# One weave of a two-layer SSM and MLP kernel reordered: halves of the w1T product in turn, the second H pair earlier, output sums first on VectorE

## The chip, the core and the metric

The kernel runs on one core of a Trainium2 chip. The metric is the device time of one execution in microseconds; less is better. The profile is of one execution, taken by the hardware profiler; times inside it count from the start of its span.

## What is computed

The reference runs a forward pass of two layers (each a state-space convolution block, then a two-matrix MLP with SiLU, both on a layer norm of the residual stream) and the gradients of all its weights and inputs but one:

```python
def _B_ref(x, w1, w2):
    return jnp.einsum("bsf,fd->bsd", _silu(jnp.einsum("bsd,df->bsf", x, w1)), w2)

x = A_q
x = x + _A_ref(_layernorm(x), A_k, A_v, A_shift_k, A_ssm_k, A_ssm_D)
x = x + _B_ref(_layernorm(x), B_w1, B_w2)
x = x + _A_ref(_layernorm(x), A_k, A_v, A_shift_k, A_ssm_k, A_ssm_D)
x = x + _B_ref(_layernorm(x), B_w1, B_w2)
# outputs: x and the vjp of x with respect to A_q, A_k, A_v, A_shift_k, A_ssm_k, A_ssm_D, B_w1, B_w2
```

There are 2048 tokens of width 448 and an inner width of 1792, all in bf16. Both layers use the same weights. `_A_ref` multiplies a layer-normed row by a convolution result y that both layers share, and adds it to the row.

## The kernel before

A prefix computes y by a matmul FFT, a main part (class `Main`) runs the two layers forward and back over four chunks of 512 tokens, and a suffix does the FFT backward, while a list of weight-gradient jobs fills the gaps. The change lies in the main part. In the code the first layer is `L = 0` and the second `L = 1`.

For a chunk the main part has these steps, each a generator that yields between pieces of TensorE work:

- `H` (line 809): the pre-activations w1 x nT in seven pairs of 128 rows, grouped 2, 3, 2 (`pairs`, line 680). The first call of a group does that pair's long products and the short "rests" (line 678) of all pairs of the group; each further call does one more pair. A pair sits in a PSUM buffer of tag `mm`, of which there are two; the fourth pair uses two buffers of tag `tr`. ScalarE reads a pair twice: SiLU into aT (line 817), and a copy into Dall (lines 818 and 116), from which `slope` (line 823) makes the derivative later. ScalarE loads a table ahead of the first SiLU and ahead of the first slope.
- `O` (line 829): for each of the chunk's four token tiles 14 matmuls of aT with w2 into a PSUM buffer of tag `po` (two buffers), in two halves of seven, then VectorE adds the sum to X (line 838). For the second layer, X goes out as the result and the upstream gradient is loaded in its place, two tiles at a time.
- `G` (line 844): the same shape as `H` with w2T and the gradient; ScalarE (and VectorE for the pairs in `dv`) evicts, and VectorE multiplies by the slope, giving the two halves of ghT (line 857, or line 980 for the second layer).
- `N` (line 860): for each of the four token tiles 14 matmuls of ghT with w1T into a `po` buffer, the first seven on ghT's first half and the last seven on its second, with a yield between; ScalarE reads the sum out into `lb_u0` (line 876), scaled, and VectorE runs two layer-norm backward steps (`_ln_bwd`, line 1027; lines 885 to 889). `lb_u0`, `lb_u1` and `gy` share three buffers of the tag `lb_u0`.
- `T` (line 894): transposes of a normed chunk on TensorE into `tr` buffers, copied to nT by ScalarE and VectorE in halves.

The order of TensorE's instructions is written out by hand (`manual_schedule` with the tensor engine alone): `weave` (line 904) takes a string and calls the named generators letter by letter. The order on VectorE, ScalarE, GpSimd and the DMA queues is made by the scheduler of the framework, which goes by program order as priority, by its own estimate of when operands are ready, and by marks: `high_priority()` puts instructions ahead of all others, `issue_after` behind a given one.

The loop over chunks (line 953) runs, for chunk c: O and G of layer 2; N of layer 2 with H of layer 1 for chunk c + 1; O of layer 1 for chunk c + 1; the forward gating and norms of layer 2 (`fwd1`, lines 768 to 777, norms from line 301 with `L308`, `L312`, `L313`, `L316`); G of layer 1; and then, for chunks 0 to 2, at line 1013, N of layer 1 with H of layer 2 for chunk c + 1:

```python
weave("NNTNNHNHNHNHNHHH", N=n, T=self.T(self.n1[1], nT, GBLK), H=self.H(c + 1, 1, nT, r))
```

In chunk 3 there is no next chunk, and N is woven with weight-gradient jobs.

## Time and profile before

| what | value |
|---|---|
| time, median of 3 runs (lowest, highest) | 695.97 us (693.32, 698.3) |
| the profiled execution's time | 692.97 us |
| its span | 690.9 us |
| TensorE matmul busy in the span | 669.0 us (97%) |
| VectorE, ScalarE, GpSimd busy | 481.6, 429.9, 104.8 us |
| granted TensorE clock | 0.999 of full |

A line of a timeline gives the start, the time until the last of its instructions ends, the engine, the line of the kernel, the operation, its output and inputs by the program's names, their sizes, and how many instructions are merged (x7). In brackets stands how long the engine had been idle before it and whose result ended that. Matmuls are pipelined: one starts well before the last has ended, so idle time in brackets is less than what the work lost, and the distance between starts says more.

| stretch of the profile before | us |
|---|---|
| N's first tile of chunk 0 to H's first step | 202.28 to 209.60 |
| H's first step to the end of the weave | 209.60 to 226.69 |
| the same two of chunk 1 start at | 293.86, 301.19 |
| and of chunk 2 | 385.45, 392.79 |

The weave takes 24.41 us in chunk 0 (202.28 to 226.69).

### The profile page before, as it was taken

To read this page: it belongs to the slowest core of one execution; us is meant where nothing else is said; L and a number is where in the kernel's file an instruction comes from. 1 tells how busy PE (TensorE), PEld (TensorE's weight loads), DVE (VectorE), ACT (ScalarE), POOL (GpSimd) and SP (SyncE) were. 2 spreads that over 40 slices of the span, in tenths; PEclk is the share of its full clock that TensorE was granted. 3 is DMA by queue.
4 is the path that set the end of the run, shared out by engine and by line. 5 is a ranking of instruction groups with operands and counts; after the bars stand their busy time and mean duration, and the time that the engine had idled before them with its cause. 6 is when DMAs were issued, how large, how long until landed. Compare 5 with 4: busy or idle time off the path is not lost.

```text
span 690.9 us, 14461 instructions
## 1 busy us (share of the span) xinstructions
PE 669.0 (97%) x5844; PEld 362.1 (52%) x5879; DVE 481.6 (70%) x1131; ACT 429.9 (62%) x522; POOL 104.8 (15%) x177
## 2 busy tenths in 40 slices
PE   8999999899999999999999999999999999999997
PEld 6876745454434444444444444544555555555666
DVE  5779943667889858899478874843936555538992
ACT  5988976878947868669577585223543543554431
POOL 1057310110011100111001000010111211102311
PEclk9999999999999999999999999999999999999999
DMA  8999978179698777597766789949599988957991
GB/s 320 244 316 321 337 203 220 56 191 259 167 265 233 221 182 176 137 253 219 199 157 183 211 231 354 271 142 210 191 249 342 328 285 315 341 190 223 320 310 42
DMA packets 203956, 162.60 MB, mean 235 GB/s; under 512 B 153505, under 2 KB 184244, under 8 KB 203122
## 3 DMA queue, kind: packets, MB, share of 16 engines
q1 hardware_dynamic: 190806, 113.35, 60.2%
q0 software_dynamic: 11088, 39.84, 16.7%
q10 hardware_dynamic: 1996, 8.49, 3.7%
q8 instruction: 46, 0.75, 0.5%
q14 instruction: 20, 0.16, 0.1%
HBM read 66.05 MB, written 54.60 MB: 175 GB/s over the span
## 4 chain that ended last, share of the span: by engine, by line
PE 64%; DVE 19%; issue 6%; ACT 5%; DMA 3%; POOL 3%; POOLq 0%; ACTq 0%
PE ps_d L1082 25%; PE ps_n L872 8%; PE ps_h L674 6%; PE ps_g L674 6%; PE ps_o L834 5%; DVE ln_st L308 2%; DVE lb_v L1030 2%; PE ps_v L272 2%; POOL rstd L313 2%; DMA spec_K<-KAB 1%; DVE n L316 1%; DVE lb_v L1033 1%; DVE lb_v L1034 1%; DVE X L838 1%; PE ps_h L678 1%
## 5 line engine op out<-in xcount | busy, mean ns | idle before, releaser
L1082 PEld LDWEIGHTS <-dstat 128*128 128x128 bf16 x928 | 87.1, 98 | 75.7 <-issue 4.0
L872 PE MATMUL ps_n<-w1T,ghT 128*128 128x448 bf16 x448 | 96.6, 353 | 2.0 <-DVE ghT L857 1.7
L834 PE MATMUL ps_o<-w2sb,aT 128*128 128x448 bf16 x448 | 89.2, 353 | 0.6 <-DVE X L838 0.6
L674 PE MATMUL ps_h<-nT,w1sb 128*128 128x512 bf16 (+1 forms) x410 | 83.5, 336 | 2.2 <-ACT Dall L116 1.0
L116 ACT CAST ghT<-ps_g 128x1024 bf16<-128x1024 f32 (+1 forms) x54 | 48.4, 900 | 58.3 <-PE ps_g L678 47.7
L674 PE MATMUL ps_g<-nT,w2T 128*128 128x512 bf16 x317 | 77.9, 379 | 2.2 <-DVE Dall L117 0.5
L872 PEld LDWEIGHTS <-ghT 128*128 128x128 bf16 x448 | 41.4, 98 | 50.7 <-DVE ghT L857 6.7
L834 PEld LDWEIGHTS <-aT 128*128 128x128 bf16 x448 | 43.2, 98 | 41.1 <-issue 2.7
L674 PEld LDWEIGHTS <-w1sb 128*128 128x128 bf16 x420 | 39.2, 98 | 36.7 <-issue 7.2
L817 ACT ACTIVATE aT<-ps_h 128x1024 bf16<-128x1024 f32 (+1 forms) x48 | 44.2, 921 | 19.1 <-PE ps_h L674 10.2
L1030 DVE SCALAR_TENSOR_TENSOR lb_v<-lb_u,n 128x448 bf16<-128x448 bf16 x60 | 37.2, 620 | 24.5 <-ACT lb_u L876 24.1
L116 ACT CAST Dall<-ps_h 128x1024 bf16<-128x1024 f32 (+2 forms) x60 | 54.3, 904 | 0.0
L313 POOL TENSOR_TENSOR rstd<-ln_ve,mhalf 128x2 f32<-128x2 f32 (+1 forms) x24 | 19.9, 831 | 225.7 <-DVE ln_ve L312 225.7
L674 PEld LDWEIGHTS <-w2T 128*128 128x128 bf16 x336 | 31.3, 98 | 42.1 <-issue 7.2
L827 ACT ACTIVATE Dall<-Dall 128x1024 bf16<-128x1024 bf16 (+1 forms) x48 | 53.2, 1186 | 0.1
L1082 PE MATMUL ps_d<-X,dstat 128*128 128x448 bf16 x224 | 47.6, 353 | 0.0
L1082 PE MATMUL ps_d<-go,dstat 128*128 128x448 bf16 x224 | 47.2, 353 | 0.0
L1082 PE MATMUL ps_d<-n3m,dstat 128*128 128x448 bf16 (+1 forms) x240 | 47.0, 340 | 0.0
L1082 PE MATMUL ps_d<-n1m,dstat 128*128 128x448 bf16 (+1 forms) x240 | 46.5, 340 | 0.0
L876 ACT ACTIVATE lb_u<-ps_n,rstd 128x448 bf16<-128x448 f32 x32 | 20.5, 640 | 28.9 <-PE ps_n L872 24.3
L116 ACT CAST A1g<-ps_v 128x1024 bf16<-128x1024 f32 x14 | 15.0, 1069 | 36.5 <-PE ps_v L272 36.5
L838 DVE TENSOR_TENSOR X<-X,ps_o 128x448 bf16<-128x448 bf16 x32 | 19.5, 611 | 21.3 <-PE ps_o L834 21.1
(210 smaller groups left out, 1112.4 us busy)
## 6 DMA issues: line engine op xcount, KB each, us to landing
dstat<-a_d SPq DMA_DIRECT2D x28, 512.0 KB, 5.2
dstat<-g_d SPq DMA_DIRECT2D x28, 512.0 KB, 5.8
a_d<-turned SPq DMA_DIRECT2D x16, 512.0 KB, 3.0
g_d<-turned SPq DMA_DIRECT2D x16, 512.0 KB, 3.0
a_d<-turned SPq DMA_DIRECT2D x16, 384.0 KB, 2.7
g_d<-turned SPq DMA_DIRECT2D x16, 384.0 KB, 3.0
spec_K<-KAB POOLq DMA_DIRECT2D x7, 512.0 KB, 5.7
KAB<-KAB POOLq DMA_DIRECT2D x28, 128.0 KB, 5.1
```

The lines of the kernel that those rows point to most:

```text
L116: return nc.scalar.copy(out, in_)
L272: nc.tensor.matmul(pv[:, r ^ (ci & 1), i, :], lhsT=src[ri, i * P:(i + 1) * P], rhs=k.Gsb[ri, g, ri], start=first, stop=not first)
L313: nc.gpsimd.tensor_tensor(out=r[:, lo:hi], in0=ve[:, lo:hi], in1=k.mhalf[:, lo:hi], op=ALU.pow)
L674: self.nc.tensor.matmul(ps, lhsT=w[:, b, ft * P:(ft + 1) * P], rhs=x[:, b], start=(start and b == 0), stop=(stop and b == bs[2]))
L817: self.last_silu = nc.scalar.activation(aT[hh][:, o:o + hi - lo, :], ps(lo, hi), ACT.Silu)
L827: self.nc.scalar.activation(dT[hh][:, o:o + n, :], dT[hh][:, o:o + n, :], ACT.Derivative_silu)
L834: nc.tensor.matmul(po[:, :D], lhsT=aT[ft // 7][:, ft % 7, tl * P:(tl + 1) * P], rhs=self.w2sb[:, ft, :], start=(ft == 0), stop=(ft == NF - 1))
L838: self.last_o = nc.vector.tensor_tensor(out=X[:, t, :], in0=X[:, t, :], in1=po[:, :D], op=ALU.add)
L872: nc.tensor.matmul(pn[:, :D], lhsT=gh[ft // 7][:, ft % 7, tl * P:(tl + 1) * P], rhs=self.w1T[:, ft, :], start=(ft == 0), stop=(ft == NF - 1))
L876: nc.scalar.activation(u0[:], pn[:, :D], ACT.Identity, scale=k.rstd[2 * L + 1][:, t:t + 1], accum_out=cp[:, tl, 0:1])
L1030: nc.vector.scalar_tensor_tensor(out=v[:], in0=u0, scalar=-1.0 / D, in1=n_t, op0=ALU.mult, op1=ALU.mult, accum_out=cp[:, 1:2])
L1082: self.nc.tensor.matmul(ps[:, cols], lhsT=st[:, t, :], rhs=mov[:, t, cols], start=(first and t == 0), stop=(last and t == NT - 1))
```

## The change

Three things change.

1. `N` gets an inner function `product(tl, h)` that does seven matmuls of tile tl with half h of ghT. For layer 1 (`L == 0`) in chunks 0 to 2 the first call does tile 0's first half, the second call tile 1's first half, the third tile 0's second half and the fourth tile 1's second half. The other tiles, layer 2 and chunk 3 go as before. There are eight calls in all, as before.
2. The string of the weave of layer 1's N with layer 2's H calls H's second step right after the first, and its sixth and seventh after the last N. With the first edit, TensorE's order from the start of the weave is: first half of tile 0, first half of tile 1, transposes, second half of tile 0, second half of tile 1, then two H steps.
3. In `O`, for the second layer and chunks 1 to 3, the sum into X is marked with `high_priority()`.

```diff
     def O(self, c, L, aT, tls=range(4)):
...
             t = 4 * c + tl
-            self.last_o = nc.vector.tensor_tensor(out=X[:, t, :], in0=X[:, t, :], in1=po[:, :D], op=ALU.add)
+            with tc.high_priority() if L == 1 and c > 0 else nullcontext():
+                self.last_o = nc.vector.tensor_tensor(out=X[:, t, :], in0=X[:, t, :], in1=po[:, :D], op=ALU.add)
...
     def N(self, c, L, gh, gres, n_b, n_a):
...
+        mix = L == 0 and c < 3
+        pns = {}
+
+        def product(tl, h):
+            if h == 0:
+                pns[tl] = k.psum.tile([P, 512], FP32, name="ps_n", tag="po", bufs=2)
+            for ft in range(7 * h, 7 * h + 7):
+                nc.tensor.matmul(pns[tl][:, :D], lhsT=gh[h][:, ft % 7, tl * P:(tl + 1) * P], rhs=self.w1T[:, ft, :], start=(ft == 0), stop=(ft == NF - 1))
+
         for tl in range(4):
...
-            pn = k.psum.tile([P, 512], FP32, name="ps_n", tag="po", bufs=2)
-            for ft in range(NF):
-                nc.tensor.matmul(pn[:, :D], lhsT=gh[ft // 7][:, ft % 7, tl * P:(tl + 1) * P], rhs=self.w1T[:, ft, :], start=(ft == 0), stop=(ft == NF - 1))
-                if ft == 6:
-                    yield
+            if not (mix and tl == 1):
+                product(tl, 0)
+                yield
+            if mix and tl == 0:
+                product(1, 0)
+                yield
+            product(tl, 1)
+            pn = pns.pop(tl)
             u0 = self.t([P, D], "lb_u0", "lb_u0", 3)
...
-                weave("NNTNNHNHNHNHNHHH", N=n, T=self.T(self.n1[1], nT, GBLK), H=self.H(c + 1, 1, nT, r))
+                weave("NNTNNHHNHNHNHNHH", N=n, T=self.T(self.n1[1], nT, GBLK), H=self.H(c + 1, 1, nT, r))
```

More of the change, by code (lines that the diff above doesn't have):

```diff
@@ L1 @@
-from contextlib import ExitStack
+from contextlib import ExitStack, nullcontext
 import numpy as np
@@ L829, in O @@
     def O(self, c, L, aT, tls=range(4)):
-        nc, k, X = self.nc, self.k, self.X
+        nc, k, X, tc = self.nc, self.k, self.X, self.tc
         for tl in tls:
```

## The prediction

> **What bounds the kernel now.** I read the page's first part, TensorE's timeline from the end of the layer-1 G product to the next G product, then VectorE and ScalarE there, then the same stretches of the next two chunks. Chunks 0, 1 and 2 of the weave that the change rewrites are called c0, c1 and c2; they start at 202.28, 293.86 and 385.45.

> ```profile
> span 690.9 us, 14461 instructions
> PE 669.0 (97%) x5844; PEld 362.1 (52%) x5879; DVE 481.6 (70%) x1131; ACT 429.9 (62%) x522; POOL 104.8 (15%) x177
> ```

> TensorE is the bound, but 97% hides its short waits: a matmul lasts 0.353 us and the next starts after 0.19, so a gap shows only when starts are compared. Its timeline in c0:

> ```profile
> 202.28 1.49 PE L872 MATMUL ps_n<-w1T,ghT 128*128 128x448 bf16 x7
> 204.08 0.36 PE L872 MATMUL ps_n<-w1T,ghT 128*128 128x448 bf16 x1 [0.32 <-DVE ghT L857]
> 204.68 1.75 PE L872 MATMUL ps_n<-w1T,ghT 128*128 128x448 bf16 x6 [0.24 <-DVE ghT L857]
> 206.37 0.64 PE L651 MATMUL ps_t<-ident,n 64*128 64x64 bf16 x32
> 206.94 2.82 PE L872 MATMUL ps_n<-w1T,ghT 128*128 128x448 bf16 x14
> 209.60 1.46 PE L674 MATMUL ps_h<-nT,w1sb 128*128 128x512 bf16 x5
> ...
> 224.27 0.39 PE L678 MATMUL ps_h<-nT,w1sb 64*128 64x512 bf16 x2
> 225.05 0.39 PE L678 MATMUL ps_h<-nT,w1sb 64*128 64x512 bf16 x2 [0.40 <-ACT Dall L116]
> 225.38 1.47 PE L674 MATMUL ps_h<-nT,w1sb 128*128 128x512 bf16 x6
> ```

> Three things are to be seen: the second half of N's first tile (204.08, 204.68) waits for ghT; the sixth H step (its last two rests, 225.05) waits for a PSUM buffer of the mm tag; and between them TensorE runs without a gap. Who is late, on VectorE and then on ScalarE:

> ```profile
> 202.99 0.70 DVE L316 TENSOR_SCALAR n<-X,ln_mv,rstd 128x448 bf16<-128x448 bf16 x2 [0.59 <-POOL rstd L313]
> 203.61 2.22 DVE L857 TENSOR_TENSOR ghT<-Dall,ghT 128x512 bf16<-128x512 bf16 x4
> ...
> 209.66 0.35 DVE L1034 TENSOR_TENSOR lb_v<-lb_v,lb_u 128x448 bf16<-128x448 bf16 x1
> ...
> 233.62 0.61 DVE L838 TENSOR_TENSOR X<-X,ps_o 128x448 bf16<-128x448 bf16 x1
> ```

> ```profile
> 206.52 0.63 ACT L876 ACTIVATE lb_u<-ps_n,rstd 128x448 bf16<-128x448 f32 x1 [3.04 <-PE ps_n L872]
> ...
> 210.12 0.63 ACT L876 ACTIVATE lb_u<-ps_n,rstd 128x448 bf16<-128x448 f32 x1 [1.97 <-DVE ln_ve L312]
> 210.66 0.19 ACT L876 ACTIVATION_READ_ACCUMULATOR lb_u<-ps_n,rstd 128x1 f32 x1
> 210.87 1.28 ACT L817 ACT_TABLE_LOAD   x1
> 212.16 1.02 ACT L817 ACTIVATE aT<-ps_h 128x1024 bf16<-128x1024 f32 x1
> 213.08 1.01 ACT L116 CAST Dall<-ps_h 128x1024 bf16<-128x1024 f32 x1
> ```

> VectorE stands still for GpSimd's rstd although ghT products are due, so its queue is in order; the last four products then run to 205.75. ScalarE reads tile 1's sum (210.12) only after L1034 of tile 0 has ended (210.01), though the sum was there by 209.76: both use the three lb_u0 buffers, in turn. Then it loads a table, and only after that evicts H's first pair.

> **The change, part by part.** *Halves in turn.* Nothing is added or removed: 14 first-half matmuls come ahead of the transposes instead of 7, the second half of tile 0 behind them. From 202.28 to 209.60 pass 7.32 us (7.33 and 7.34 in c1, c2); the work is four half products at 1.33 (211.53 to 212.86 is one) and the transposes at 0.58, 5.90 together. 1.4 us a chunk are lost. Afterwards the transposes come at 204.94 and the second half of tile 0 at 205.52; its sixth matmul, the first that needs the last product, comes at 206.47, and that product ends at 205.75. The transposes need n, ready at 203.69, and both nT copies get 2.66 us before H starts at 208.18, as before. So the cover is 0.7 us, and all of the 1.4 goes; were it short, the loss would come back by what is missing. Gain 3 x 1.4 = 4.2.

> *The second pair sooner.* The order H H N H N H N H N H H puts a half product (1.33) between the fifth and sixth H steps and takes it from between the first and second. The fifth and sixth steps start at 221.58 and 225.38, 3.80 apart, for 1.30 + 1.93 of work (1.93 is the first step, 209.60 to 211.53): 0.57 lost, and 1.33 of cover ends it. Gain 3 x 0.57 = 1.7. With the first part: 2.0 a chunk.

> *What is late next.* The third H step needs the buffer of the first pair. On TensorE it now comes a half product earlier, and tiles 0 and 1 end 1.33 apart instead of 3.2. With c0's clock: tile 0's sum is read at about 207.1 (0.09 after its end, as at 206.52), read out by 207.85; L1030 to L1034 take 1.42 (c2: 390.48 to 392.50, less the nT copy of 0.60 within it), so tile 1's is read at 209.35, read out at 210.08; table load to 211.38; Silu and the copy to Dall take 1.93 (212.16 to 214.09), so the buffer is free at 213.35. TensorE wants it at 208.18 + 1.93 + 1.30 + 1.33 = 212.74. New wait: 0.6, and some 0.1 at the fifth buffer, which the next 1.83 of ScalarE frees. In c0 and c1 VectorE also has four bn_stats of the next chunk's rows (0.59 each) in hand, which c2 lacks; on average half of one stands in the way, so I take 1.0 there and 0.7 in c2. Not above 1.8: 0.7 and a pair of bn_stats (1.14). Not below 0: if ScalarE evicts the first pair ahead of tile 1's sum, its table load starts at 207.85 and nothing waits. I take the middle because before had the sum first in all three chunks.

> *Output sums first on VectorE.* Same 12 instructions of 0.61 us. At 233.62 the sum of chunk 1's tile 0 runs, whose matmuls ended near 229.5; the third O tile waits for its buffer, 0.31 by the waits, 0.38 by starts (0.92 after the rests at 233.37, against 0.54 between rests and next step at 210.99), once more at 325.88, and not in chunk 3, where the sums already run 2.65 apart as TensorE delivers them. Gain 2 x 0.38 = 0.76. What they overtake on VectorE is the tail of the layer-norm backward and the LN of the next chunk, needed at 247.46 (n is done at 235.4): nothing. The stores on GpSimd's queue and reloads of X on SP's keep their count of two a chunk; they may be issued up to 4 us sooner, with no reader before N of layer 2 (249.32). At worst, each sum holds VectorE; that is a rival.

> *Where ScalarE takes part back.* After H it evicts the last pair, loads a table, runs six slopes (6.64) and only then evicts G's first pair, done at 237.66 where TensorE needs it at 238.23: slack 0.57. If H ends g sooner, its fifth pair's eviction starts at the end of its matmuls and the last Dall copy is ready g - 0.38 sooner (1.93 + 1.83 after 224.65 for g = 1.0, against 228.82). So c0 and c1 yield the lesser of g + 0.38 and g - 0.38 + 0.57: with g = 2.0 - 1.0, 1.2. In c2 the first G pair waits for that copy (412.06): g - 0.38 with g = 1.3, 0.9.

> Sum: 1.2 + 1.2 + 0.9 = 3.3 us. The profiled execution took 692.97 (span 690.9 and 2.07 around it), so 689.7 for its like; the median of the runs shown is 695.97, 3.0 above it, and there it is 692.7. Behind 432 TensorE has no gaps but the same work, which only moves up.

> [...] On ScalarE the read-out ends at 210.85, the load starts at 210.87 and Silu at 212.16: a switch of tables costs 1.3 us. [...]

> **Rivals.**
> 1. VectorE's bn_stats stand ahead of L1034 in full: new wait 1.8 in c0 and c1. There g = 0.2, 0.4 each; with 0.9, a gain of 1.7: 694.3. For it: L1030 came at 208.00, 0.75 after its input. Against: nT's copy now fills part of that time.
> 2. ScalarE takes H's first pair ahead of tile 1's sum: no new wait, g = 2.0; 2.2 + 2.2 + 1.6 = 6.0: 690.0. For it: H's first pair ends only 0.8 after that sum can be read. Against: all three chunks of before.
> 3. Slower: the sums stand in VectorE's queue ahead of their matmuls. One mechanism, at chunks 1 and 2: if the first two are each a tile early (2.65), VectorE stands for 5.3 us; its cast of G's second pair starts at 236.05 + 5.3 and ends at 242.6, where TensorE needs that buffer at 240.05. It decides from 2.75 us a chunk (1.05 idle before the cast, 1.7 from its end to the need). 2 x 2.5 lost, 0.9 gained in c2: 700.1. For it: VectorE does stand for rstd and for ps_g (1.05). Against: the sums come 3 to 4 us after their matmuls now.
> 4. VectorE becomes the bound in c0 and c1 (15.95 busy of 17.09 from 209.60) and gives nothing back: 0.9, 695.1. Against: none of what it does late there is read before 247.
> 5. The table switch stalls ScalarE longer once work waits behind it: a second load's 1.28 more in all three chunks leaves 0.2, 695.8. Against: both switches in c0 are followed by work 0.01 us later. [...]
> That the wait for ghT doesn't go at all is excluded by the 0.7 of cover.

> **How the numbers follow.** Forecast 0.50 (692.7); rivals in order 0.20, 0.16, 0.05, 0.06, 0.03. The three runs of before lie 5 apart, so a median may stand 2.5 off: from rival 2 less 2.5 to rival 1 plus 2.5, 687.5 to 697, which leaves out rival 3 and the tails, under 2 in 10. A measurement of this kernel tells about 1% from no change. Faster by over 1% is below 689.0: nearly half of rival 2 and a little of the forecast, 0.10. Slower by over 1% is above 702.9: the upper part of rival 3, 0.03. Within: 0.87.

> **What would show it.** Right: no L872 wait on ghT L857, the transposes 2.7 us behind the first ps_n, no wait at the sixth H step, L838 within 0.3 of its matmuls, and a wait of the third H step for Dall of 0.6 to 1.0. No such wait means rival 2; over 1.5, rival 1. VectorE idle in front of L838 means rival 3. I am wrong if another order on VectorE or ScalarE, anywhere in the three chunks, makes a new wait that these rows don't show.

## The result, and the profile after

| what | before | after |
|---|---|---|
| median of 11 runs each (lowest, highest) | 695.49 us (693.32, 698.33) | 700.25 us (697.65, 704.02) |
| the profiled execution's time, span | 692.97, 690.9 | 700.64, 698.8 |
| granted TensorE clock in it | 0.999 | 0.995 |

The changed kernel takes 1.0068 times as long (95% interval 1.0047 to 1.0089): slower by 0.7%, where 692.7 was forecast with a range to 697.0. The signs promised for the first two edits came, but the new wait, foreseen at 0.6 to 1.0 us, is 3.36. The sign of the third did not: the output sums of chunks 1 and 2 were to start within 0.3 us of their matmuls' end, and the first three of each start 1.22, 2.50 and 1.18 after it (in before 4.13, 3.29 and 1.19). The head of the page after:

```profile
span 698.8 us, 14494 instructions
PE 672.7 (96%) x5879; PEld 362.9 (52%) x5879; DVE 483.4 (69%) x1131; ACT 429.6 (61%) x522; POOL 104.8 (15%) x177
```

The largest of TensorE's waits in the main part after (engine, line, waited for: us in total, times, longest):

```profile
PE ps_h L674 <- ACT Dall L116: 8.3, 6, 3.4
```

The three old waits, of line 872 (now 873) for ghT, of line 678 for Dall and of line 834 for X, are gone from this list. H steps of line 674 that wait for Dall, 1.0 us in all before, stand at its top instead. TensorE in c0 after:

```profile
205.50 2.81 PE L873 MATMUL ps_n<-w1T,ghT 128*128 128x448 bf16 x14
208.24 0.64 PE L651 MATMUL ps_t<-ident,n 64*128 64x64 bf16 x32
...
212.15 1.47 PE L674 MATMUL ps_h<-nT,w1sb 128*128 128x512 bf16 x6 [0.51 <-DVE nT L117]
...
220.24 1.73 PE L674 MATMUL ps_h<-nT,w1sb 128*128 128x512 bf16 x6 [3.36 <-ACT Dall L116]
221.91 1.46 PE L678 MATMUL ps_h<-nT,w1sb 64*128 64x512 bf16 x6
```

The halves in turn work: the transposes start 2.74 us after N, and nothing waits for ghT. Then H's first step waits 0.51 for nT, and its third 3.36 for ScalarE; c1 has the same two waits to the hundredth, c2 no wait for nT and 0.60 at the third step. And at 221.91 the six rests take 1.46 us, where the same six take 0.84 in c1: the granted clock was 0.50. The granted clock by stretches of the profile after (us of the stretch, busy time by engine, then PEclk); the last is c1's same wait:

```profile
221.30:224.70 3.40, 3.40 (x12) 0.86 (x11) 2.92 (x10) 2.65 (x3) 0.08 (x1) 0.50 0.68 154
...
310.00:325.00 15.00, 11.64 (x60) 5.30 (x59) 14.17 (x48) 12.34 (x18) 0.58 (x1) 1.00 0.85 208
```

Who is late? VectorE in c0 after:

```profile
208.97 1.15 DVE L308 BATCH_NORM_STATS2 ln_st<-w1sb 128x6 f32<-128x448 bf16 x2
...
211.44 0.66 DVE L117 COPY nT<-ps_t 128x1024 bf16<-128x1024 bf16 x1
...
213.33 0.70 DVE L316 TENSOR_SCALAR n<-w1sb,ln_mv,rstd 128x448 bf16<-128x448 bf16 x2 [1.16 <-POOL rstd L313]
...
214.56 0.62 DVE L1043 SCALAR_TENSOR_TENSOR lb_v<-lb_u,n 128x448 bf16<-128x448 bf16 x1
...
215.72 0.39 DVE L1047 TENSOR_TENSOR lb_v<-lb_v,lb_u 128x448 bf16<-128x448 bf16 x1
```

And ScalarE:

```profile
210.88 0.19 ACT L889 ACTIVATION_READ_ACCUMULATOR lb_u<-ps_n,rstd 128x1 f32 x1
216.23 0.63 ACT L889 ACTIVATE lb_u<-ps_n,rstd 128x448 bf16<-128x448 f32 x1 [5.15 <-DVE lb_v L1047]
...
216.97 1.28 ACT L817 ACT_TABLE_LOAD   x1
218.26 1.02 ACT L817 ACTIVATE aT<-ps_h 128x1024 bf16<-128x1024 f32 x1
```

For the order that these replace, three lines of VectorE before:

```profile
207.49 0.59 DVE L308 BATCH_NORM_STATS2 ln_st<-w2sb 128x6 f32<-128x448 bf16 x1
208.00 0.60 DVE L1030 SCALAR_TENSOR_TENSOR lb_v<-lb_u,n 128x448 bf16<-128x448 bf16 x1
...
211.37 0.40 DVE L316 TENSOR_SCALAR n<-w1sb,ln_mv,rstd 128x448 bf16<-128x448 bf16 x1 [0.93 <-POOL rstd L313]
```

Here is the new order. Tile 0's sum is read out at 211.07. Before, VectorE ran four bn_stats of the next chunk's rows, then tile 0's first backward step (L1030 at 208.00 to L1034, now L1043 to L1047), and only after it the normed rows n (L316, first at 211.37). After, all of that norm stands ahead: four bn_stats, a wait of 1.16 for GpSimd's rstd, and four n (1.32 us to 214.65). The backward step starts 3.5 us after its input was there; 2.5 of that are the wait for rstd and the four n, which came behind it before. ScalarE, which needs the lb_u0 buffer that L1047 releases, stands for 5.15 us; behind that stand the table load and the eviction of H's first pair, and behind these TensorE. The bn_stats also stand ahead of nT's copy, which is the wait of 0.51. In c2 there is no next chunk to norm, and the wait is 0.60, as forecast.

Starts of layer 1's N and of the O that follows it cut the main part, from c0's start to c2's end, into pieces that add up. "Weave" is N's first matmul to the next O's first, "rest" from there to the next layer-1 N, so it holds the other weaves of the chunk; the last columns add the five differences to before, and give the difference of the medians. All in us; the experiments' kernels stand in the same table.

| kernel | weave c0 | c1 | c2 | rest after c0 | after c1 | sum to before | medians to before |
|---|---|---|---|---|---|---|---|
| before | 24.41 | 24.42 | 26.93 | 67.17 | 67.17 | | |
| after | 28.28 | 26.71 | 25.99 | 66.88 | 66.88 | +4.64 | +4.76 |
| halves_only | 27.53 | 25.96 | 25.56 | 66.83 | 66.82 | +2.60 | +2.23 |
| string_sums | 23.85 | 24.12 | 26.57 | 66.88 | 66.88 | -1.80 | -1.66 |
| four_bufs | 23.18 | 23.18 | 25.21 | 67.52 | 67.52 | -3.49 | -3.49 |
| norm_held | 22.49 | 22.49 | 25.98 | 69.71 | 69.72 | +0.29 | +2.17 |
| early_table | 25.27 | 25.27 | 25.21 | 66.88 | 66.88 | -0.59 | -0.02 |
| held_no_sums | 22.48 | 22.48 | 25.99 | 71.36 | 69.67 | +1.88 | +1.84 |
| bufs_held | 22.49 | 22.48 | 25.21 | 66.88 | 66.88 | -6.16 | -6.11 |
| bufs_no_sums | 23.17 | 23.17 | 25.21 | 68.27 | 68.27 | -2.01 | -1.63 |
| keep_busy | 26.71 | 26.72 | 25.99 | 66.89 | 66.89 | +3.09 | +3.76 |
| nt_held | 22.48 | 22.49 | 25.99 | 66.89 | 66.88 | -5.38 | -6.66 |

The profiled executions lie 7.9 us of span apart. 4.64 of that is the change; 3.22 is there before the first weave starts (202.28 against 205.50), in a stretch that the change leaves alone; the last section says what it is.

### The profile page after: what moved, and what is told of

Its sections match the earlier page's. It is cut to its first block, busy times and chain, and to the rows that moved or that the text cites. A ratio compares the mean times of both kernels' runs of the same rounds, so it can differ in the third digit from the quotient of the medians.

```text
span 698.8 us, 14494 instructions
## 1 busy us (share of the span) xinstructions
PE 672.7 (96%) x5879; PEld 362.9 (52%) x5879; DVE 483.4 (69%) x1131; ACT 429.6 (61%) x522; POOL 104.8 (15%) x177
## 4 chain that ended last, share of the span: by engine, by line
PE 73%; DVE 10%; DMA 6%; ACT 5%; issue 3%; POOL 3%; ACTq 0%; POOLq 0%; DVEq 0%; SPq 0%
PE ps_d L1095 25%; PE ps_n L873 9%; PE ps_o L834 8%; PE ps_h L674 8%; PE ps_g L674 7%; PE ps_v L272 2%; DMA spec_KV<-ZkvB 2%; PE ps_h L678 2%; PE ps_g L678 2%; DVE ln_st L308 2%; DMA turned<-ghT 1%; ACT Dall L116 1%; POOL rstd L313 1%; PE ps_gK L1378 1%; DVE n L316 1%
## 5 line engine op out<-in xcount | busy, mean ns | idle before, releaser
L873 PE MATMUL ps_n<-w1T,ghT 128*128 128x448 bf16 x448 | 95.1, 355 | 0.0
L674 PE MATMUL ps_h<-nT,w1sb 128*128 128x512 bf16 (+1 forms) x420 | 85.2, 338 | 10.0 <-ACT Dall L116 8.3
L116 ACT CAST ghT<-ps_g 128x1024 bf16<-128x1024 f32 (+1 forms) x54 | 48.3, 899 | 57.4 <-PE ps_g L678 45.7
L674 PE MATMUL ps_g<-nT,w2T 128*128 128x512 bf16 x336 | 80.0, 381 | 1.1 <-DVE Dall L117 0.5
L674 PEld LDWEIGHTS <-w1sb 128*128 128x128 bf16 x420 | 38.8, 98 | 47.2 <-issue 17.1
L1043 DVE SCALAR_TENSOR_TENSOR lb_v<-lb_u,n 128x448 bf16<-128x448 bf16 x60 | 37.3, 621 | 27.8 <-ACT lb_u L889 27.4
L817 ACT ACTIVATE aT<-ps_h 128x1024 bf16<-128x1024 f32 (+1 forms) x48 | 44.2, 921 | 19.1 <-PE ps_h L674 11.4
L116 ACT CAST Dall<-ps_h 128x1024 bf16<-128x1024 f32 (+2 forms) x60 | 54.4, 907 | 0.0
L313 POOL TENSOR_TENSOR rstd<-ln_ve,mhalf 128x2 f32<-128x2 f32 (+1 forms) x24 | 19.7, 820 | 228.7 <-DVE ln_ve L312 228.7
L674 PEld LDWEIGHTS <-w2T 128*128 128x128 bf16 x336 | 31.5, 98 | 42.8 <-issue 8.4
L116 ACT CAST A1g<-ps_v 128x1024 bf16<-128x1024 f32 x14 | 14.9, 1065 | 36.5 <-PE ps_v L272 36.5
```

What stands on the lines that cost most here:

```text
L116: return nc.scalar.copy(out, in_)
L313: nc.gpsimd.tensor_tensor(out=r[:, lo:hi], in0=ve[:, lo:hi], in1=k.mhalf[:, lo:hi], op=ALU.pow)
L674: self.nc.tensor.matmul(ps, lhsT=w[:, b, ft * P:(ft + 1) * P], rhs=x[:, b], start=(start and b == 0), stop=(stop and b == bs[2]))
L817: self.last_silu = nc.scalar.activation(aT[hh][:, o:o + hi - lo, :], ps(lo, hi), ACT.Silu)
L873: nc.tensor.matmul(pns[tl][:, :D], lhsT=gh[h][:, ft % 7, tl * P:(tl + 1) * P], rhs=self.w1T[:, ft, :], start=(ft == 0), stop=(ft == NF - 1))
L1043: nc.vector.scalar_tensor_tensor(out=v[:], in0=u0, scalar=-1.0 / D, in1=n_t, op0=ALU.mult, op1=ALU.mult, accum_out=cp[:, 1:2])
```

## The experiments

**The theory, A:** with the first edit VectorE gets the next chunk's norm ahead of tile 0's backward step, so that ScalarE's second read-out waits for a lb_u0 buffer, and H's first pair is evicted late. The rivals look elsewhere: in the other two edits, in ScalarE's own work, in VectorE's load, in the priority of the sums. Letters in the expectations are those of the theories as each of them describes it. Each kernel's median is set against the runs of before beside it (695.33, 694.97 or 694.88).

**halves_only**: the first edit alone.

```diff
-            with tc.high_priority() if L == 1 and c > 0 else nullcontext():
+            with tc.high_priority() if False else nullcontext():
-                weave("NNTNNHHNHNHNHNHH", ...)
+                weave("NNTNNHNHNHNHNHHH", ...)
```

> The first edit alone: halves in turn, the old string, no priority for the sums. Theory A (VectorE takes the norm of the next chunk's rows ahead of tile 0's backward step in c0 and c1, so ScalarE, which needs one of the three lb_u0 buffers back, evicts H's first pair some 3.5 us later): VectorE's order is that of the whole change, the third H step comes one half product (1.33) later than with the new string, so it waits about 2.0 us in c0 and c1 instead of 3.36 and not at all in c2; the 1.4 is gained in each chunk, 0.5 to 0.7 lost at nT in c0 and c1. Sum: about 1.5 us slower than before, 697. Rival B (the new string makes the wait, by taking a half product from ahead of the third H step): no wait at the third H step with the old string, 4.2 us gained, 691.

Measured: 697.56 against 695.33, ratio 1.0029 (1.0004 to 1.0054). Already slower, with the same order on VectorE. TensorE's timeline in c0:

```profile
209.51 1.47 PE L674 MATMUL ps_h<-nT,w1sb 128*128 128x512 bf16 x6 [0.51 <-DVE nT L117]
...
217.61 1.67 PE L674 MATMUL ps_h<-nT,w1sb 128*128 128x512 bf16 x6 [2.04 <-ACT Dall L116]
```

The third H step starts 8.10 us after the first here, and 8.09 in after: ScalarE sets the time, whatever stands between. The old string has one half product (1.33) more ahead of it, and 3.36 less 1.33 is about the 2.04 that it waits. So the second edit gained nothing there: it moved work from before the wait to behind it. With the 0.57 that it gains at the sixth step, it makes the weave 0.75 longer in c0 and c1 (28.28 against 27.53, 26.71 against 25.96): the two edits work against each other, and the slowdown isn't the sum of what each does alone.

**string_sums**: the second and third edits without the first.

```diff
-        mix = L == 0 and c < 3
+        mix = False
```

> The second and third edits without the first: new string, sums first, whole tiles as before. Theory A: VectorE keeps the order of before, H's first pair is free at 214.09 on the clock of before and the third H step wants it at 214.16, so no wait there, none at the sixth H step and none for L838: 0.57 a chunk and 0.38 twice gained, 2.5 us, 693. Rival B (the string makes the wait): 3 us of new wait in c0 and c1, 699 or more.

Measured: 693.67 against 695.33, ratio 0.9976 (0.9955 to 0.9996). No wait at the third H step, the wait for ghT is back (1.7 us over six times), and VectorE has the order of before in the weave. The two edits are a small gain by themselves; with the first edit beside them the sign turns.

**four_bufs**: after, with four lb_u0 buffers for three. The order of the instructions on each engine is that of after; only ScalarE's second read-out need no longer wait for tile 0's backward step.

```diff
-            u0 = self.t([P, D], "lb_u0", "lb_u0", 3)
+            u0 = self.t([P, D], "lb_u0", "lb_u0", 4)
...
-                gy = self.t([P, D], "gy", "lb_u0", 3)
+                gy = self.t([P, D], "gy", "lb_u0", 4)
```

> The whole change with four lb_u0 buffers instead of three; the order of all engines' instructions is unchanged, only the wait of ScalarE's second read-out for L1047 of tile 0 falls away. Theory A: ScalarE reads tile 1's sum as soon as it is there, the wait of 3.36 at the third H step (and 0.60 in c2) goes, 0.5 at nT stays; on TensorE the weave gains about 1.3 in c0 and c1 and 2.0 in c2 over before, and the time is 690 to 692. Rival C (VectorE's later backward steps bound the weave through any buffer, a po or lb_u0 one): the wait only moves to a later N or H step and the time stays above 697.

Measured: 691.84 against 695.33, ratio 0.9948 (0.9929 to 0.9968). The wait at the third H step is gone in all three chunks, and with it 5.1 us of c0's weave, 3.5 of c1's and 0.8 of c2's. That settles the buffer as the link between VectorE and ScalarE. The two waits of 0.5 for nT stay, as VectorE's order does. A new wait comes behind, 0.9 in all, when O of layer 2 waits for its sum: TensorE arrives sooner, VectorE doesn't.

**norm_held**: after, with the next chunk's norm held on VectorE until the end of tile 0's first backward step.

```diff
+            lb = _ln_bwd(k, self.ch, u0[:], n_b[:, tl, :], cp[:, tl, :], gres(tl), Gt)
+            if L == 0 and tl == 0:
+                self.last_lb = lb
...
-                with tc.issue_after((self.last_g if c else self.last_dv).ins):
+                with tc.issue_after((self.last_lb if c else self.last_dv).ins):
```

> The whole change, and VectorE's norm of the next chunk's rows (c0 and c1) queued behind tile 0's first backward step by issue_after. The scheduler then also puts SiLU of H's first pair ahead of tile 1's read-out on ScalarE. Theory A: L1047 of tile 0 ends some 3.5 us sooner, the wait at the third H step is under 0.7 in all three chunks, and nT's 0.5 goes too: 690 to 692. Rival C: VectorE has the same work, 15.95 of 17.09 us busy in c0, and its end is only moved; G of layer 2 or its transposes wait for the norm that was held, and the time stays above 694.

Measured: 697.50 against 695.33, ratio 1.0016 (0.999 to 1.0042), a miss. The weave is mended (22.49), but the rest is 2.8 us longer than in after. TensorE there, in chunk 1's O and G:

```profile
241.89 0.39 PE L678 MATMUL ps_g<-nT,w2T 64*128 64x512 bf16 x2 [2.03 <-DVE ghT L117]
```

VectorE and GpSimd of the same kernel:

```profile
239.38 1.32 DVE L316 TENSOR_SCALAR n<-X,ln_mv,rstd 128x448 bf16<-128x448 bf16 x4 [2.07 <-POOL rstd L313]
240.61 1.22 DVE L117 CAST ghT<-ps_g 128x1024 bf16<-128x1024 f32 x1
```

```profile
237.23 0.54 POOL L841 DMA_DIRECT2D out_dram<-X  x1 [13.24 <-DVE g L1050]
...
238.31 1.04 POOL L313 TENSOR_TENSOR rstd<-ln_ve,mhalf 128x4 f32<-128x4 f32 x1
```

The norm is now done so late that it meets the next stage: VectorE has written its variances by 237.31, GpSimd first issues two stores (the second at 237.76) and has rstd at 239.35, and VectorE stands for 2.07 us, though the last matmul of G's second pair, whose cast it runs only behind the four n, had ended at 236.70. The table's sum says +0.29 and the medians +2.17: the profiled execution (694.66, clock 1.0) is one of the quicker of its twelve; nine of the others show 0.994 to 0.997, and where their clock fell was not traced.

**held_no_sums**: norm_held without the third edit.

```diff
-            with tc.high_priority() if L == 1 and c > 0 else nullcontext():
+            with tc.high_priority() if False else nullcontext():
```

> norm_held without the third edit. In norm_held VectorE stood 2.07 us for rstd, because GpSimd's queue had the store of X ahead of it; without the priority of the sums the scheduler puts rstd ahead of that store. Theory E (the early sums cost by way of GpSimd's queue): VectorE's wait for rstd falls to about 1.0, the cast of G's second pair comes 1 us sooner in chunks 1 and 2, 695.5. Rival F (VectorE is full there, and the sums without priority come later still): the O step's third tile waits for its buffer 1 us or more, and nothing is gained, 697.5 or more.

Measured: 696.81 against 694.97, ratio 1.0026 (0.9999 to 1.0053). TensorE's wait of 2.03 for the cast, which in norm_held lies behind VectorE's 2.07 for rstd, is gone, as theory E expected in kind; but nothing is gained. Its place is taken by a larger wait of O for its sums. The rest after c1 is as long (69.67 against 69.72). From TensorE's waits:

```profile
PE ps_o L834 <- DVE X L839: 5.6, 2, 2.8
```

VectorE has the whole of the norm to do there, and what comes behind it, cast or sum, is late. Both kernels say that the norm may be held, but not for so long.

**early_table**: after, with ScalarE's table for SiLU loaded right behind tile 0's read-out, by a SiLU of four elements a row that nobody reads (added work).

```diff
+            if mix and tl == 0:
+                with self.tc.issue_after(rd.ins):
+                    nc.scalar.activation(k.warm[:], k.mhalf[:], ACT.Silu)
```

> The whole change, and a SiLU of four columns queued on ScalarE right behind tile 0's read-out in c0, c1 and c2, so that the table load (1.28 us) falls into ScalarE's idle time ahead of tile 1's read-out instead of behind it; VectorE's order is unchanged. Theory A (the wait is the chain lb_u0 buffer, read-out, table load, eviction of the first pair): 1.28 less wait at the third H step in c0 and c1 (2.1 instead of 3.4) and none in c2 (0.6): about 3 us off the whole change, 697. Rival D (ScalarE loads the table on its own ahead of the SiLU and the load is hidden): no difference, 700.

Measured: 694.95 against 694.97, ratio 0.9983 (0.996 to 1.0007). ScalarE and TensorE in c0:

```profile
210.37 1.28 ACT L892 ACT_TABLE_LOAD   x1
```

```profile
218.09 1.46 PE L674 MATMUL ps_h<-nT,w1sb 128*128 128x512 bf16 x6 [1.93 <-ACT Dall L116]
```

The load falls into ScalarE's idle time ahead of its second read-out, and the wait is 1.43 shorter in c0 and c1 and gone in c2: the load lay on the path. The weave of c0 is shorter by 3.0, not 1.4, since the granted clock is 1.00 there (215 to 225) and not 0.50.

**keep_busy**: after, with 16 matmuls of 448 columns into an unread `tr` buffer ahead of the third H step in c0 and c1. This is added work, to ask what the clock costs.

```diff
+    def W(self):
+        pw = self.k.psum.tile([P, 512], FP32, name="ps_w", tag="tr", bufs=2)
+        for i in range(16):
+            self.nc.tensor.matmul(pw[:, :D], lhsT=self.w1sb[:, i % 3, 0:P], rhs=self.w2sb[:, i % NF, :], start=True, stop=True)
+        yield
...
-                weave("NNTNNHHNHNHNHNHH", ...)
+                weave("NNTNNHHNWHNHNHNHH" if c < 2 else "NNTNNHHNHNHNHNHH", ...)
```

> The whole change, and in c0 and c1 16 further matmuls of 448 columns on TensorE ahead of the third H step, into a tr buffer that nobody reads: added work of some 3.0 us that lies inside the wait of 3.4, so that TensorE isn't idle there. All other engines' orders stay. Theory K (a wait of 3.4 us also costs the clock: the changed kernel's trace shows it at half for 3.4 us from 221.29, behind the wait that ends at 220.24, and the next matmuls 1.7 us late): the granted clock comes back to 0.998 or more and the time falls by 1.5 to 3 us, 697.5 to 699. Rival L (the half clock is chance, or costs nothing): 700 or more, since the matmuls are added work.

Measured: 698.64 against 694.88, ratio 1.0041 (1.0016 to 1.0067). TensorE's timeline in c0:

```profile
216.61 3.19 PE L914 MATMUL ps_w<-w2sb,w1sb 128*128 128x448 bf16 x16
220.13 1.46 PE L674 MATMUL ps_h<-nT,w1sb 128*128 128x512 bf16 x6 [0.33 <-ACT Dall L116]
```

The third H step starts 4.85 us after the half product ahead of it (215.28), as in after (215.39 to 220.24), so the useless matmuls only fill the wait. But c0's weave takes 26.71 for after's 28.28, exactly what c1 takes in either kernel. The granted clock of keep_busy is 1.00 from 205 to 240; the half clock in c0 of after costs 1.57 us. The two kernels' medians differ by 1.6 as well, but their intervals against before overlap, so the weaves carry this. Over all executions the granted clock averages 0.998 here and 0.995 in after, which fits.

**bufs_held**: both remedies together, four lb_u0 buffers and the norm held, but only until VectorE's copy of nT has been issued. **nt_held**: the same hold with three buffers, so VectorE's order alone.

```diff
-            _copy(nc, (engs or (nc.scalar, nc.vector))[r], dv[:, :, :, r, :], pts[r])
+            self.last_nt = _copy(nc, (engs or (nc.scalar, nc.vector))[r], dv[:, :, :, r, :], pts[r])
...
-                with tc.issue_after((self.last_g if c else self.last_dv).ins):
+                with tc.issue_after((self.last_nt if c else self.last_dv).ins):
```

> four_bufs, and VectorE's norm of the next chunk's rows queued behind its half of the nT copy. Theory A: the wait of H's first step for nT (0.5 by the waits, 0.7 by starts) goes in c0 and c1, tile 0's backward step comes 3 us sooner, no new wait: 1.2 us off four_bufs, 690.6. Rival C (VectorE's work is only moved to the O step of layer 2 and comes back there as in norm_held): 693 or more.

> bufs_held with three lb_u0 buffers as in the change: only VectorE's norm of the next chunk's rows is held behind nT's copy. Theory M (in c0 and c1 the order on VectorE is the cause, and with it mended the third buffer comes back in time): no wait at the third H step in c0 and c1, 0.6 in c2, 0.7 us over bufs_held, 689.6. Rival N (the fourth buffer is what cures): a wait of 0.6 or more in all three chunks, 691 or more.

Measured: bufs_held 688.86 against 694.97, ratio 0.9901 (0.9864 to 0.9938); nt_held 688.22 against 694.88, ratio 0.9883 (0.9851 to 0.9915). These two, of six runs each, are the fastest of the study, about 1% below before, and the runs don't tell them apart. VectorE and TensorE of nt_held in c0:

```profile
206.53 0.68 DVE L117 COPY nT<-ps_t 128x1024 bf16<-128x1024 bf16 x1
...
208.79 0.60 DVE L1043 SCALAR_TENSOR_TENSOR lb_v<-lb_u,n 128x448 bf16<-128x448 bf16 x1
...
210.36 0.37 DVE L1047 TENSOR_TENSOR lb_v<-lb_v,lb_u 128x448 bf16<-128x448 bf16 x1
```

```profile
213.59 1.46 PE L674 MATMUL ps_h<-nT,w1sb 128*128 128x512 bf16 x6
```

H's third step starts 4.56 us after its first (209.03), with no wait at either. And ScalarE:

```profile
210.86 1.02 ACT L817 ACTIVATE aT<-ps_h 128x1024 bf16<-128x1024 f32 x1 [0.92 <-PE ps_h L678]
211.78 0.63 ACT L889 ACTIVATE lb_u<-ps_n,rstd 128x448 bf16<-128x448 f32 x1
```

It takes H's first pair ahead of tile 1's sum: the order of the forecast's second rival, in c0 and c1; in c2 the sum goes first and 0.6 is waited. One hold on VectorE's order turns 4.8 us of loss into 6.7 of gain by the medians, 4.6 into 5.4 by the table; so the order is the cause and the buffer only its link. The hold changed ScalarE's order with it, in c0 and c1. C2 of after parts the two: VectorE has no norm there and ScalarE keeps the old order, and 0.60 is waited. So 2.76 of the 3.36 are VectorE's order.

**bufs_no_sums**: four_bufs without the third edit, to see what that is worth.

> four_bufs without the third edit. Theory G: VectorE is some 3 us later with its backward steps than before, and a sum without priority stands behind all of them, so the third O tile of chunks 1 and 2 waits for its buffer 2 to 3 us more than with priority: 695 to 697. Rival H (the third edit is worth the 0.38 a chunk that before lost): 0.8 more than four_bufs, 692.6.

Measured: 693.34 against 694.97, ratio 0.9971 (0.9946 to 0.9996). Between the two expectations. O's wait for its sum is 1.4 us a chunk for four_bufs' 0.4, and the rest 68.27 for 67.52: the priority is worth 0.75 a chunk here.

## Why the prediction was wrong, step by step

- **Halves in turn**, 1.4 a chunk: right. The transposes start 2.74 us after N where they started 4.09 after it: 1.35. "Both nT copies get 2.66 us before H starts" was wrong in c0 and c1. VectorE's copy came behind four bn_stats, and 0.67 was given back (H starts 6.65 after N, not 5.98 as in c2).
- **The second pair sooner**, 0.57 a chunk: the wait at the sixth H step is gone. Where nothing else changes in the weave, in string_sums, it gains 0.30 to 0.56. Ahead of a wait that ScalarE sets, the half product that it takes away from the third step is lost again: against halves_only, the weave of after is 0.75 longer in c0 and c1.
- **What is late next** is the step that failed: "New wait: 0.6", 1.0 taken in c0 and c1, "Not above 1.8". It measured 3.36 in both, and 0.60 in c2, where 0.7 was taken. The sum took VectorE's order of before for given and let at most a pair of bn_stats stand in the way. What stands in the way is the whole norm, with a wait for GpSimd inside it: four bn_stats, 1.16 idle, four n. By c0's working L1034 was to end at 209.27, 1.1 us after H's start; after, L1047 ends at 216.11, 4.0 after it.
- **The clock** was in no term: 1.57 us in c0, by after's c0 against its c1 and against keep_busy.
- **Output sums**, 0.38 twice: the rest is 0.29 shorter, but the edit isn't needed for it. It is 0.34 shorter in halves_only, which lacks the edit; that the late weave lets VectorE catch up there is argued, not tried. Nor does the mark put a sum directly behind its matmuls: in after they still start up to 2.50 us late. String_sums has the 0.29 too, with no late weave, so there the edit may be its cause. Its worth is parted from the rest only without the long wait (0.75 a chunk, four_bufs against bufs_no_sums).
- **Where ScalarE takes part back**: never reached in after, since nothing was gained. In nt_held c0 and c1 give 1.93 and 0.29 each, where rival 2 worked out 2.2.

So c0: 1.35 and 0.57 gained, 0.67, 3.52 (by starts: the third step comes 4.85 after a half product of 1.33) and 1.57 lost: 3.84 by sum, 3.87 by the table. c1: the same without the clock, 2.27 against 2.29.

Rival 1 named the right engine and the right place, with half the price: it counted bn_stats, not the norm behind them. Its "over 1.5" was the sign that came. Rival 2 was right about c0 and c1 of the kernel with the order mended: 6.0 by its working, 5.4 by the table and 6.7 by the medians; in c2 the sum still goes first, and 0.94 was gained for its 1.6. Rivals 3 and 4 show nowhere in after: its rests are 0.29 shorter than before's. Rival 5, a longer table switch, is excluded: SiLU starts 0.01 us after the load, and early_table gets back 1.43 for a load of 1.28.

The last sentence of the prediction, that another order on VectorE could make a wait which the rows don't show, describes what happened, but it had no price and no chance in the sum. That the time lies within 1% of before, to which 0.87 was given, is luck: a gain was forecast and a loss came.

Three slips in the working change little. The H step that starts at 225.38 is the seventh, not the sixth; the 0.57 stands. The last ghT product ends at 205.83 by its line (203.61 and 2.22), not 205.75, so the cover was 0.64. And 1.93 + 1.83 after 224.65 is 228.41, which is 0.41 ahead of 228.82 and not the 0.62 that g - 0.38 gives; with 0.2 less a chunk the forecast gain would have been 2.7 us for 3.3.

Why the scheduler puts the norm first is not shown. The first edit moves tile 0's last matmuls behind tile 1's first half, so that tile 0's backward step becomes ready later by its own estimate; that is argued from the code, and was not tried.

## What to carry to other kernels

A reordering of one engine's instructions is also an input to whatever orders the others: before adding up what a moved step gains, ask which instructions on the other engines are ready in the gap that it opens, and price the whole group that could slip in, with any wait inside it (here the norm, with 1.16 us of waiting for rstd). When a buffer links two engines, as lb_u0 does here, compare three remedies: hold the intruder for a short time, add a buffer, or move what stands behind it into the idle time; here a short hold was worth most (nt_held, ratio 0.9883; four buffers 0.9948, the early table 0.9983), and a hold past the whole backward step gave it all back (1.0016). A string of the schedule that depends on another engine's release is worth only what stands behind that release.

## What the runs showed of the hardware that was not expected

**The clock fell to half at eight of sixteen short waits.** The twelve profiles have sixteen idle stretches of TensorE of 1.9 us or more. Eight of them, of 2.01 to 4.3 us, go with a stretch at a granted clock of 0.50, which lasts 3.4 us in six cases and 6.8 in two (string_sums and bufs_no_sums, in the first chunk, with a mean clock of 0.995 each). The 3.36 in c0 of after and the 2.04 in halves_only's c0 are among the eight; the same 3.36 in c1 of after, the 2.04 in halves_only's c1, a 2.80 in held_no_sums' next chunk and a 3.1 in early_table's first chunk are not. Where it fell in a weave or behind one it cost 1.57 (after, halves_only) or 1.69 (held_no_sums: 71.36 less 69.67), about half of the stretch.

**The first chunk waits for a store for a time that varies.** On VectorE, ahead of the first norm of a stage that no edit touches, in the profile of after:

```profile
89.98 0.63 DVE L721 TENSOR_TENSOR X<-x0c,a_t 128x896 bf16<-128x896 bf16 x1 [2.98 <-DMA spec_KV<-ZkvB]
```

TensorE waits for the rows normed there 2.0 us (line 662, up to 94.00), and the clock falls at 95.0. VectorE stands 0.71 there in before. TensorE doesn't wait at that place in before and bufs_held; it waits 0.7 in nt_held, 3.0 in string_sums and 4.3 in bufs_no_sums. This follows no edit, as none touches what comes ahead of it. So 3.22 of the 7.9 us between the two profiled spans is no part of the change.

**GpSimd's two stores held its rstd back by 1.0 us** (norm_held: its input ready at 237.31, started at 238.31), and VectorE's queue stood behind it. So two DMA issues of 0.54 us each are half of VectorE's 2.07, behind which TensorE waited 2.03 for the cast.
